# Where the softmax sums of the memory rows stand in an attention segment, and in which array shape they are taken

## The chip, the cores and the metric

The kernel runs on one core of a Trainium2 chip. The metric is the device time of one execution in microseconds (us). The engines of the core have short names here: PE is TensorE (matrix products; PEld is its loading of stationary operands, "weights"), DVE is VectorE, ACT is ScalarE, POOL is GpSimd, SP is SyncE, which issues most transfers. Each engine works through its own instructions in the order of the program; they wait for one another by semaphores.

## The reference

Two kinds of blocks alternate, A, B, A, B, each added to a residual of 2048 rows by 512 columns. B is a gated feed-forward block. A, which the change touches, is a recurrent attention with a memory of 8 rows, run over 64 segments of 32 rows, one after another, with 32 heads of 128 columns:

```python
for s in range(n_seg):
    xs = x[:, s * seg_len:(s + 1) * seg_len, :].copy()
    h = jnp.concatenate([mem, xs], axis=1)
    q = jnp.einsum('btd,dhe->bhte', h, Wq)
    k = jnp.einsum('btd,dhe->bhte', h, Wk)
    v = jnp.einsum('btd,dhe->bhte', h, Wv)
    scores = jnp.einsum('bhqe,bhke->bhqk', q, k) * scale
    scores = jnp.where(mask[None, None], scores, -1000000000.0)
    p = _softmax(scores, axis=-1)
    o = jnp.einsum('bhqk,bhke->bhqe', p, v)
    o = jnp.einsum('bhte,hed->btd', o, Wo)
    mem = o[:, :M, :].copy()
    outs.append(o[:, M:, :])
```

The 8 memory rows of a segment's output are the next segment's memory. So each segment has to wait for the memory rows of the one before it, while its 32 token rows are wanted only later.

## The kernel before

The function `segment(s, ...)` writes one of the 128 segments (64 in each A block). The order on PE, DVE and ACT is the order in which the program names the instructions (`manual_schedule`), so what stands earlier in the code runs earlier on its engine.

The 32 heads are cut into two halves, r = 0 and r = 1, of 16 heads. Within a half the sixteen heads lie in two groups g of 64 partitions. One segment runs as follows; line numbers are those of the profile.

- `qk` (matmuls in `mm_chunk`, L762) projects queries and keys; ACT copies them out (L1087) and DVE turns them (L1090) into QQ and KA. `v_mm` (also L762) projects the values of a half in four parts of four matmuls each, 128 rows by 512 columns, of which four run side by side on 32 columns of the array each. This use of the array is called the 32-column shape below.
- `scores(r)` (L1113, L1117) writes the scores of a half into the PSUM tile psS. `exps(r)` on ACT (L1122) takes their exponential into S, and `close(r)` on DVE (L1125) multiplies with the mask into E[:, r]. E holds, with the keys on the partitions, the unnormalised probabilities.
- The values of half 0 are copied out of PSUM by DVE (L1211, VA[:, 0]), those of half 1 by ACT out of the tile psW (L1226, VA[:, 1]; the profile calls psW psV).
- `fill()` takes the next piece of work that doesn't depend on the segment (projections of a later block, output products of an earlier one): three times in a segment, four matmuls at the first place, eight or four at the second, sixteen or more at the third.
- `pv(r)` multiplies E with the values (L1162, eight matmuls; L1165, two more) into psO[r]. These matmuls take 64 rows of the array each, two side by side, one for each group g: the 64-row shape.
- The softmax's denominators are column sums of E, taken by matmuls with a matrix of ones. `sums_tokens` (L1154, four matmuls, 64-row shape) gives those of the token queries of both halves in the tile psT. For the 8 memory queries half 0 has `sums_zero` (L1136): sixteen matmuls in the 32-column shape with the constant `half`, two for each group and each 32 columns, into columns 224 to 351 of psS. They stand between the third and the fourth part of half 1's values. Half 1 has `sums_one` (L1145): four matmuls in the 64-row shape into columns 320 to 383 of psO[1].
- `inverse(r, src)` makes the reciprocal of the memory sums on ACT as a logarithm (L1179) and an exponential with scale -1 (L1180) into Rm. `memory_out(r)` on DVE (L1183) multiplies psO[r] with it into uT.
- `wo_pairs` (L945) multiplies the memory rows of half 0's sixteen heads with Wo into px, and `wo_rest` (L952) those of half 1. Their sum is the next segment's memory.
- Later ACT inverts the token sums of psT (L1262, L1265) and DVE applies them (L1186, L1189).

The tiles psQ, psS and psT share one place in PSUM (the pool `att`, one buffer): psT can't be written before the last reader of psS is done.

On ACT, between half 1's exponential and the copy of half 1's values, stands half 0's logarithm:

```python
invert = inverse(0, pN.rearrange("p (g q) -> p g q", g=2))
nc.scalar.copy(VA[:, 1].rearrange("p i e -> p (i e)"), psW[:])
invert()
close(1)
```

Where two accesses of a tile touch different banks or columns, the kernel says so by `other_bank`, and no wait is made; so it is for `sums_zero`, which is told not to wait for the exponential of half 1 (`other_bank(sums_zero(pN), expd)`).

Of the kernel before, what the change touches and what calls it, by code (L numbers as in the profile page):

```python
# [7 lines left out]
BF16 = mybir.dt.bfloat16  # L8
# [6 lines left out]
P = 128  # L15
# [52 lines left out]
def _consts(ctx, tc, c, b_sp, between):  # L68
    nc = tc.nc
    cp = ctx.enter_context(tc.tile_pool(name="consts", bufs=1))  # L70
    bsp = cp.tile([P, 16], F32, name="bsp")
    tctx = ExitStack()
    tmp = tctx.enter_context(tc.tile_pool(name="consts_tmp", bufs=1))
    maskf = tmp.tile([P, 224], F32, name="maskf")
    nc.gpsimd.memset(maskf[:], 1.0)
    fourth = tmp.tile([P, 4, 32], F32, name="fourth")
    nc.gpsimd.memset(fourth[:], 0.0)
    nc.gpsimd.affine_select(out=fourth[:], in_=fourth[:], compare_op=ALU.not_equal, fill=1.0,
                            base=0, pattern=[[-1, 4], [-4, 32]], channel_multiplier=1)
    own = maskf[:, 160:224].rearrange("p (i q) -> p i q", i=4)  # L80
    is_own = tmp.tile([P, 4, 1], F32, name="is_own")
    nc.vector.tensor_reduce(out=is_own[:], in_=fourth[:], op=ALU.max, axis=mybir.AxisListType.X)
    nc.vector.tensor_copy(own, is_own[:].to_broadcast([P, 4, 16]))
    between()
    for q in range(0, P, 32):
        blk = maskf[q:q + 32, 0:160].rearrange("p (i q) -> p i q", i=4)[:, :, 8:32]
        nc.gpsimd.affine_select(out=blk, in_=blk, compare_op=ALU.is_ge, fill=0.0, base=8,
                                pattern=[[0, 4], [1, 24]], channel_multiplier=-1)
        last = own[q:q + 32, :, 8:16]
        nc.gpsimd.affine_select(out=last, in_=last, compare_op=ALU.is_ge, fill=0.0, base=0,  # L90
                                pattern=[[1, 4], [4, 8]], channel_multiplier=-1)
    maskN = cp.tile([P, 2, 224], BF16, name="maskN")
    nc.vector.memset(maskN[:], 0.0)
    for gs in range(4):
        nc.vector.tensor_copy(maskN[32 * gs:32 * gs + 32, gs % 2, :], maskf[32 * gs:32 * gs + 32, :])
    ones = cp.tile([P, P], BF16, name="ones")
    nc.vector.memset(ones[:], 1.0)
    half = cp.tile([P, 2, 32], BF16, name="half")
    nc.vector.memset(half[:], 0.0)
    for g in range(2):  # L100
        nc.vector.memset(half[64 * g:64 * g + 64, g, :], 1.0)
    bsp_bf = cp.tile([P, 16], BF16, name="bsp_bf")

    def load_bsp():
        nc.vector.memset(bsp_bf[:], 0.0)
        nc.sync.dma_start(bsp_bf[:], b_sp.rearrange("(t p) -> p t", p=P))
        return lambda: nc.vector.tensor_copy(bsp[:], bsp_bf[:])

    c["bsp"], c["load_bsp"] = bsp, load_bsp
    tctx.close()  # L110
    c.update(maskN=maskN, ones=ones, half=half)
    return c


# [510 lines left out]
def cols_rhs(w, j, kt, cg):  # L625
    at = 2048 * (j % 2) + 512 * cg
    return w[j // 2][:, kt, at:at + 512]
# [90 lines left out]
def a_block(tc, c, rows, front, MV_in, RS_in, MV_out, RS_out, ahead, wo, S, first):  # L718
    nc = tc.nc
    NSEG = S // SEG  # L720
    NB = S // P
    scale = float(DH) ** -0.5
    maskN, ones, half = c["maskN"], c["ones"], c["half"]

    with ExitStack() as ctx:

# [33 lines left out]
        def mm_chunk(ps, lhs, rhs, kts=range(KT)):  # L760

            return [nc.tensor.matmul(ps[32 * cg:32 * cg + 32, :], lhsT=lhs(kt, cg), rhs=rhs(kt, cg), start=(kt == 0), stop=(kt == KT - 1),  # L762
                                     tile_position=(0, 32 * cg)) for kt in kts for cg in range(4)]

        def other_bank(mms, *reads):

            for m in mms:
                for r in reads:
                    tc.declare_no_dep(m.ins, r.ins, reason="another bank of the tile")
# [300 lines left out]
        def segment(s, fill, spare1, spare2, spare3, tail, loads):  # L1070
# [4 lines left out]
            VA = vsp.tile([P, 2, 4, DH], BF16, name="VA")  # L1075
# [6 lines left out]
            E = segp.tile([P, 2, 2, 224], BF16, name="E", bufs=1)  # L1082
# [9 lines left out]
            def v_mm(r, ps, kts=range(KT)):  # L1092
                return mm_chunk(ps, lambda kt, cg: hA_cur[:, kt, :], lambda kt, cg: cols_rhs(w, 4 + r, kt, cg), kts)

            def ends(q):

                return q.rearrange("p h (b e) -> p h b e", e=8)[:, :, 0:5:4, :]
# [5 lines left out]
            def heads40(q):  # L1103
                return q.rearrange("p (i q) -> p i q", q=40)
# [16 lines left out]
            def exps(r):  # L1121
                return nc.scalar.activation(out=S[:, r], in_=psS[:, r, 0:224], func=ACT.Exp, scale=scale)  # L1122

            def close(r):
                nc.vector.tensor_tensor(out=E[:, r], in0=S[:, r].unsqueeze(1).to_broadcast([P, 2, 224]), in1=maskN[:], op=ALU.mult)  # L1125

            def e_all(e, lo, hi):

                return e[:, :, 0:160].rearrange("p n (i q) -> p n i q", q=40)[:, :, :, lo:hi]

            def e_own(e, b):
                return e[:, :, 160:224].rearrange("p n (i b e) -> p n i b e", i=4, b=2)[:, :, :, b, :]

            def sums_zero(pN):

                return [nc.tensor.matmul(pN[32 * cg:32 * cg + 32, 64 * g:64 * g + 64], lhsT=half[:, g, :], rhs=e_own(E[:, 0], 0) if k else e_all(E[:, 0], 0, 8),  # L1136
                                         start=False, stop=True, tile_position=(0, 32 * cg), skip_group_check=True)
                        for k in range(2) for g in range(2) for cg in range(4)]

            def sums_one():  # L1140

                for k in range(2):
                    for g in range(2):
                        e = E[64 * g:64 * g + 64, 1]
                        nc.tensor.matmul(psO[1][:, g, 320:384], lhsT=ones[64 * g:64 * g + 64, :], rhs=e_own(e, 0) if k else e_all(e, 0, 8),  # L1145
                                         start=(k == 0), stop=True, skip_group_check=True)

            def sums_tokens(ps):

# [7 lines left out]
            def pv(r):  # L1157

                for i in range(4):
                    for g in range(2):  # L1160
                        o = psO[r][:, g, 0:320].rearrange("p (s i q) -> p s i q", s=2, i=4)[:, :, i, :]
                        nc.tensor.matmul(o, lhsT=VA[64 * g:64 * g + 64, r, i, :], rhs=E[64 * g:64 * g + 64, r, :, 40 * i:40 * i + 40],  # L1162
                                         start=(r == 0 and i == 0), stop=True, skip_group_check=True)
                for g in range(2):
                    nc.tensor.matmul(ends(heads40(psO[r][:, g, 0:320])), lhsT=VX[64 * g:64 * g + 64, j4, r, :],  # L1165
                                     rhs=E[64 * g:64 * g + 64, r, :, 160:224], start=False, stop=True, skip_group_check=True)
# [10 lines left out]
            def inverse(r, src):  # L1177
                rm = Rm[:, r]
                nc.scalar.activation(out=rm, in_=src, func=ACT.Ln)  # L1179
                return lambda: nc.scalar.activation(out=rm, in_=rm, func=ACT.Exp, scale=-1.0)  # L1180

            def memory_out(r):
                nc.vector.tensor_tensor(out=hview(uT_cur[:], r, 24, 32), in0=oview(r, 0, 8), in1=Rm[:, r].rearrange("p g (n q) -> p g n q", q=8), op=ALU.mult)  # L1183
# [21 lines left out]
            psS = att.tile([P, 2, 512], F32, name="psS")  # L1205
            scores(0)
            expd = exps(0)
# [8 lines left out]
            psW = accB.tile([P, 512], F32, name="psV")  # L1216
            v_mm(1, psW, (0, 1))
            other_bank(scores(1), expd)
            expd = exps(1)
            v_mm(1, psW, (2,))  # L1220
            pN = psS[:, 0, 224:352]
            other_bank(sums_zero(pN), expd)
            v_mm(1, psW, (3,))
            Rm = segp.tile([P, 2, 2, 64], F32, name="Rm", bufs=1)
            invert = inverse(0, pN.rearrange("p (g q) -> p g q", g=2))
            nc.scalar.copy(VA[:, 1].rearrange("p i e -> p (i e)"), psW[:])  # L1226
            invert()
            close(1)

            psO = [attO[r].tile([P, 2, 512], F32, name="psO") for r in range(2)]  # L1230
            if not begin:
                fill()
            pv(0)
            psT = att.tile([P, 2, 512], F32, name="psT")
            sums_tokens(psT)
            sums_one()
            pv(1)
            memory_out(0)
            spare1(E)
            if not begin:  # L1240
# [62 lines left out]
        start = nc.vector if first else nc.gpsimd  # L1303
# [138 lines left out]
        for i in range(H // 2):  # L1442
            for k in range(4):
                h = 2 * i + k % 2
                nc.tensor.matmul(pw[32 * k:32 * k + 32, :], lhsT=ends[k // 2][:, h, :], rhs=wo.head(h).rearrange("p (kt g el) -> p g kt el", kt=4, g=4),
                                 start=(i == 0), stop=(i == H // 2 - 1), tile_position=(0, 32 * k))
# [46 lines left out]
```

## Time and profile before

| | |
|---|---|
| time, median of three runs | 1605.64 us (1602.85 to 1606.57) |
| the profiled execution, device time | 1610.6 us |
| its span in the trace | 1608.9 us |
| PE busy | 1579.1 us (98% of the span) |
| ACT, DVE, POOL busy | 1052.3, 1070.4, 306.5 us |
| the two A blocks, 36 to 697 us and 822 to 1470 us | PE busy 651.3 of 661 us and 643.2 of 648 us |
| granted PE clock | 1.00 in all stretches |

A segment takes some 10 us. In the profile a busy PE only says that some matmul was in flight: a matmul's record is longer than its share of the stream. So the records of four matmuls of 512 columns, 0.40 us, overlap with those of the next four, which start 0.21 us later. What a group costs PE is read from one start to the next, not from the lengths.

A line of the timeline gives the start in us, the length in us, the engine, the line of the kernel, the operation, what it writes and reads with shapes, and how many like it were merged. In brackets is the idle time of the engine before it, and what ended it. Idle time of PEld is not idle time of PE: weights are loaded ahead.

### The profile page before, as it was taken

To read this page: it belongs to the slowest core of one execution; us is meant where nothing else is said; L and a number is where in the kernel's file an instruction comes from. 1 tells how busy PE (TensorE), PEld (TensorE's weight loads), DVE (VectorE), ACT (ScalarE), POOL (GpSimd) and SP (SyncE) were. 2 spreads that over 40 slices of the span, in tenths; PEclk is the share of its full clock that TensorE was granted. 3 is DMA by queue.
4 is the path that set the end of the run, shared out by engine and by line. 5 is a ranking of instruction groups with operands and counts; after the bars stand their busy time and mean duration, and the time that the engine had idled before them with its cause. 6 is when DMAs were issued, how large, how long until landed. Compare 5 with 4: busy or idle time off the path is not lost.

```text
span 1608.9 us, 90911 instructions
## 1 busy us (share of the span) xinstructions
PE 1579.1 (98%) x41021; PEld 981.3 (61%) x41046; DVE 1070.4 (67%) x3066; ACT 1052.3 (65%) x2279; POOL 306.5 (19%) x674
## 2 busy tenths in 40 slices
PE   7899999999999999999999999999999999999999
PEld 3566666666666666666656666666666766665565
DVE  4667766677777776784466666666677667768622
ACT  4677777777777777670057777777777777776400
POOL 6211111112211221320011111111122122224000
PEclk9999999999999999999999999999999999999999
DMA  9322112222311332378952212212233223426698
GB/s 364 131 57 46 40 44 44 50 42 82 80 43 40 87 86 61 106 172 175 209 162 45 48 44 50 44 47 46 73 92 73 47 72 92 97 54 178 143 194 164
DMA packets 255773, 149.67 MB, mean 93 GB/s; under 512 B 188504, under 2 KB 231104, under 8 KB 255384
## 3 DMA queue, kind: packets, MB, share of 16 engines
q1 hardware_dynamic: 241464, 97.68, 27.4%
q0 software_dynamic: 13920, 46.18, 8.9%
q8 instruction: 321, 5.26, 1.4%
q14 instruction: 68, 0.56, 0.1%
HBM read 60.21 MB, written 39.55 MB: 62 GB/s over the span
## 4 chain that ended last, share of the span: by engine, by line
PE 92%; DMA 5%; issue 1%; DVE 1%; ACT 1%; POOL 1%; SPq 0%; POOLq 0%; DVEq 0%; ACTq 0%
PE psQ L762 13%; PE psK L762 13%; PE psb L762 9%; PE pg L403 9%; PE psO L952 7%; PE px L945 7%; PE psm L762 7%; PE psV L762 7%; PE pwB L964 3%; PE psO L1162 3%; PE pz L302 3%; PE py L446 2%; PE psT L1154 2%; PE psS L1113 2%; DMA Wk_sb<-in_A_Wk_dram 1%
## 5 line engine op out<-in xcount | busy, mean ns | idle before, releaser
L762 PEld LDWEIGHTS <-hT 128*32 128x32 bf16 x12288 | 345.3, 96 | 259.2 <-DVE hT L1062 17.7
L762 PE MATMUL psV<-Wv_sb,hT 128*32 128x512 bf16 x2048 | 166.4, 379 | 0.0
L1087 ACT CAST rows<-psQ 128x512 bf16<-128x512 f32 x256 | 145.4, 588 | 23.2 <-PE psQ L762 19.4
L1183 DVE TENSOR_TENSOR uT<-psO,Rm 128x128 bf16<-128x128 f32 x256 | 74.6, 291 | 123.6 <-ACT Rm L1180 123.4
L1090 DVE STREAM_TRANSPOSE QQ<-rows 128x256 f32<-128x256 f32 x256 | 112.5, 439 | 66.2 <-ACT rows L1087 63.6
L1122 ACT ACTIVATE S<-psS 128x224 bf16<-128x224 f32 x256 | 92.2, 360 | 98.1 <-PE psS L1117 98.1
L1090 DVE STREAM_TRANSPOSE KA<-rows 128x256 f32<-128x256 f32 x256 | 113.0, 441 | 64.9 <-ACT rows L1087 62.4
L403 PE MATMUL pg<-z,wspT 128*128 128x344 bf16 x1024 | 154.3, 309 | 0.0
L762 PE MATMUL psK<-Wv_sb,hT 128*32 128x512 bf16 x2048 | 153.2, 378 | 0.0
L1186 DVE TENSOR_TENSOR uT<-psO,Rt 128x384 bf16<-128x384 f32 x256 | 139.9, 547 | 16.4 <-ACT Rt L1265 14.4
L1265 ACT ACTIVATE Rt<-Rt 128x512 f32<-128x512 f32 x256 | 147.3, 622 | 4.0
L952 PE MATMUL psO<-Wo_high,uT 128*32 128x128 bf16 x8192 | 143.0, 219 | 4.1 <-issue 2.2
L762 PE MATMUL psQ<-Wq_sb,hT 128*32 128x512 bf16 x2048 | 136.4, 379 | 0.2 <-issue 0.2
L762 PE MATMUL psQ<-Wk_sb,hT 128*32 128x512 bf16 x2048 | 136.2, 379 | 0.0
L762 PE MATMUL psK<-Wk_sb,hT 128*32 128x512 bf16 x2048 | 136.0, 379 | 0.0
L762 PE MATMUL psm<-Wq_sb,hT 128*32 128x512 bf16 x2048 | 136.0, 379 | 0.0
L945 PE MATMUL px<-Wo,uT 128*32 128x256 bf16 x3840 | 133.8, 273 | 1.3 <-issue 1.2
L952 PEld LDWEIGHTS <-uT 128*32 128x32 bf16 x8192 | 123.6, 97 | 16.2 <-issue 7.8
L403 PEld LDWEIGHTS <-wspT 128*128 128x128 bf16 x1024 | 100.1, 98 | 53.4 <-issue 0.4
L1262 ACT ACTIVATE Rt<-psT 128x1024 f32<-128x1024 f32 x127 | 130.1, 1024 | 3.1
L945 PEld LDWEIGHTS <-uT 128*32 128x32 bf16 x4096 | 104.5, 97 | 25.2 <-issue 2.6
L1044 POOL COPY KX<-old 128x128 bf16<-128x128 bf16 x128 | 65.5, 539 | 263.8 <-PE psS L1117 170.7
(224 smaller groups left out, 2892.9 us busy)
## 6 DMA issues: line engine op xcount, KB each, us to landing
o_d<-o_sb SPq DMA_DIRECT2D x126, 64.0 KB
vb_d<-front SPq DMA_DIRECT2D x31, 256.0 KB
VX<-vb_d SPq DMA_DIRECT2D x124, 64.0 KB
ln_x<-xd SPq DMA_DIRECT2D x26, 256.0 KB
y_o<-o_d POOLq DMA_DIRECT2D x22, 256.0 KB, 3.4
xd<-y_o POOLq DMA_DIRECT2D x22, 256.0 KB, 3.2
Wq_sb<-in_A_Wq_dram POOLq DMA_DIRECT2D x8, 512.0 KB, 7.1
Wk_sb<-in_A_Wk_dram POOLq DMA_DIRECT2D x8, 512.0 KB, 9.3
```

The lines of the kernel that those rows point to most:

```text
L403: nc.tensor.matmul(pg[t][:, k, 0:344], lhsT=wsp[t][:, st, :], rhs=z(st, 344 * k, 344 * k + 344), start=(st == 0), stop=(st == NT - 1))
L762: return [nc.tensor.matmul(ps[32 * cg:32 * cg + 32, :], lhsT=lhs(kt, cg), rhs=rhs(kt, cg), start=(kt == 0), stop=(kt == KT - 1), tile_posi ...
L945: nc.tensor.matmul(px[at:at + 32, 0:256], lhsT=lhs[:, h, :], rhs=wo_rhs(h, slice(k + 2, None, -2) if h % 2 else slice(k, None, 2)), start= ...
L952: nc.tensor.matmul(pw[32 * cg:32 * cg + 32, :], lhsT=lhs[:, h, :], rhs=wo_rhs(h, cg), start=False, stop=(h == H - 1), tile_position=(0, 32 ...
L1044: eng.tensor_copy(KX[r][:].rearrange("p g (k i) -> p i g k", i=4), bs["KTB"][:, r].rearrange("p (i g) k -> p i g k", i=4)[:, :, :, 8 * j4: ...
L1087: return r, mms, copy(r[:].rearrange("p (n el two) -> p n el two", n=8, two=2), ps.rearrange("p (n two el) -> p n el two", n=8, two=2))
L1090: nc.vector.transpose(out=(QQ[:, j % 2, :, 0:32] if j < 2 else KA[:, j % 2]).bitcast(F32).rearrange("p n q one -> p n (q one)"), in_=r[:]. ...
L1122: return nc.scalar.activation(out=S[:, r], in_=psS[:, r, 0:224], func=ACT.Exp, scale=scale)
L1183: nc.vector.tensor_tensor(out=hview(uT_cur[:], r, 24, 32), in0=oview(r, 0, 8), in1=Rm[:, r].rearrange("p g (n q) -> p g n q", q=8), op=ALU ...
L1186: nc.vector.tensor_tensor(out=hview(uT_nxt[:], r, 0, 24), in0=oview(r, 8, 32), in1=rview(r, 0, 24), op=ALU.mult)
L1262: nc.scalar.activation(out=Rt[:], in_=psT[:], func=ACT.Ln)
L1265: nc.scalar.activation(out=rt, in_=rt, func=ACT.Exp, scale=-1.0)
```

## The change

Half 0's memory sums no longer stand between two parts of the values' projection, in sixteen matmuls of the 32-column shape, but as four matmuls of the 64-row shape at the head of the stretch of `pv` and sums, ahead of `pv(0)`. One function, `sums_memory`, serves both halves. The token sums move from the middle of that stretch to its end, behind `pv(1)`. On ACT the copy of half 1's values comes directly after half 1's exponential, and half 0's logarithm and exponential follow it. `close(1)` is named before the sums, `inverse(0)` after `pv(0)`. The declaration that the sums need not wait for the exponential goes, and so does the constant `half`.

```diff
-    half = cp.tile([P, 2, 32], BF16, name="half")
-    nc.vector.memset(half[:], 0.0)
-    for g in range(2):
-        nc.vector.memset(half[64 * g:64 * g + 64, g, :], 1.0)
...
-            def sums_zero(pN):
-
-                return [nc.tensor.matmul(pN[32 * cg:32 * cg + 32, 64 * g:64 * g + 64], lhsT=half[:, g, :], rhs=e_own(E[:, 0], 0) if k else e_all(E[:, 0], 0, 8),
-                                         start=False, stop=True, tile_position=(0, 32 * cg), skip_group_check=True)
-                        for k in range(2) for g in range(2) for cg in range(4)]
-
-            def sums_one():
+            def sums_memory(r, ps, begun):
 
                 for k in range(2):
                     for g in range(2):
-                        e = E[64 * g:64 * g + 64, 1]
-                        nc.tensor.matmul(psO[1][:, g, 320:384], lhsT=ones[64 * g:64 * g + 64, :], rhs=e_own(e, 0) if k else e_all(e, 0, 8),
-                                         start=(k == 0), stop=True, skip_group_check=True)
+                        e = E[64 * g:64 * g + 64, r]
+                        nc.tensor.matmul(ps[:, g, :], lhsT=ones[64 * g:64 * g + 64, :], rhs=e_own(e, 0) if k else e_all(e, 0, 8),
+                                         start=(k == 0 and not begun), stop=True, skip_group_check=True)
...
             expd = exps(1)
-            v_mm(1, psW, (2,))
-            pN = psS[:, 0, 224:352]
-            other_bank(sums_zero(pN), expd)
-            v_mm(1, psW, (3,))
+            v_mm(1, psW, (2, 3))
+            close(1)
+            nc.scalar.copy(VA[:, 1].rearrange("p i e -> p (i e)"), psW[:])
             Rm = segp.tile([P, 2, 2, 64], F32, name="Rm", bufs=1)
-            invert = inverse(0, pN.rearrange("p (g q) -> p g q", g=2))
-            nc.scalar.copy(VA[:, 1].rearrange("p i e -> p (i e)"), psW[:])
-            invert()
-            close(1)
 
             psO = [attO[r].tile([P, 2, 512], F32, name="psO") for r in range(2)]
             if not begin:
                 fill()
+            sums_memory(0, psS[:, :, 224:288], True)
             pv(0)
+            inverse(0, psS[:, :, 224:288])()
+            sums_memory(1, psO[1][:, :, 320:384], False)
+            pv(1)
             psT = att.tile([P, 2, 512], F32, name="psT")
             sums_tokens(psT)
-            sums_one()
-            pv(1)
             memory_out(0)
             spare1(E)
```

## The prediction

> **What bounds the kernel now.** I read the busy times and the chain of work that ended last first:
>
> ```profile
> PE 1579.1 (98%) x41021; PEld 981.3 (61%) x41046; DVE 1070.4 (67%) x3066; ACT 1052.3 (65%) x2279; POOL 306.5 (19%) x674
> ...
> PE 92%; DMA 5%; issue 1%; DVE 1%; ACT 1%; POOL 1%; SPq 0%; POOLq 0%; DVEq 0%; ACTq 0%
> ```
>
> PE is the bound, and 92% of the chain lies on it. So the question is what the change does to PE's stream in one segment, times 128. For that I read the timeline of one ordinary segment, where each line is a group of like instructions:
>
> ```profile
> 344.84 0.68 DVE L1211 CAST VA<-psK 128x512 bf16<-128x512 f32 x1
> ...
> 345.12 0.30 PE L1136 MATMUL psS<-E,half 128*32 128x64 bf16 x16
> 345.17 0.36 ACT L1122 ACTIVATE S<-psS 128x224 bf16<-128x224 f32 x1 [0.75 <-PE psS L1117]
> ...
> 345.24 0.40 PE L762 MATMUL psV<-Wv_sb,hT 128*32 128x512 bf16 x4
> ...
> 345.45 0.40 PE L964 MATMUL pwB<-Wo_high,front 128*32 128x512 bf16 x4
> 345.49 0.28 ACT L1179 ACTIVATE Rm<-psS 128x128 f32<-128x128 f32 x1
> 345.56 0.39 DVE L1125 TENSOR_TENSOR E<-S,maskN 128x448 bf16<-128x448 bf16 x1
> 345.69 0.58 ACT L1226 CAST VA<-psV 128x512 bf16<-128x512 f32 x1
> ...
> 345.79 0.32 PE L1162 MATMUL psO<-E,VA 64*128 64x80 bf16 x8
> ...
> 345.94 0.22 PE L1165 MATMUL psO<-E,VX 64*128 64x128 bf16 x2
> ...
> 346.01 0.45 PE L1154 MATMUL psT<-E,ones 64*128 64x512 bf16 x4
> 346.17 0.31 ACT L1180 ACTIVATE Rm<-Rm 128x128 f32<-128x128 f32 x1
> ...
> 346.30 0.22 PE L1145 MATMUL psO<-E,ones 64*128 64x64 bf16 x4
> ...
> 346.36 0.31 PE L1162 MATMUL psO<-E,VA 64*128 64x80 bf16 x8
> ...
> 346.50 0.22 PE L1165 MATMUL psO<-E,VX 64*128 64x128 bf16 x2
> 346.51 0.29 DVE L1183 TENSOR_TENSOR uT<-psO,Rm 128x128 bf16<-128x128 f32 x1 [0.56 <-ACT Rm L1180]
> ...
> 346.65 0.40 PE L964 MATMUL pwB<-Wo_high,front 128*32 128x512 bf16 x4
> ...
> 346.88 1.04 PE L945 MATMUL px<-Wo,uT 128*32 128x256 bf16 x30
> ```
>
> The reader is to see three things. First, what groups cost from start to start: L1136's sixteen matmuls 0.12 us (345.12 to 345.24), L1145's four 0.06, eight of L1162 0.15, the token sums 0.29, and four fills 0.21. Second, two gaps: from the first fill's end (345.66) to pv(0) 0.13 us, which isn't the wait for half 0's values (their copy ended at 345.52) and which I take as the price of entering the 64-row shape; and at the way out 0.09 (346.50 to 346.65, less 0.06 for two matmuls). Third, how tight half 1 is: E[:, 1] ends at 345.95 and the token sums start 0.06 later; the copy of half 1's values ends at 346.27, and pv(1) starts at 346.36. Between those two events stand the token sums and sums_one: 0.35 us of PE work that need only E.
>
> How long PE takes to go on after a wait is seen in a segment without a first fill:
>
> ```profile
> 77.01 0.11 PEld L1154 LDWEIGHTS <-ones 64*128 64x128 bf16 x4 [0.22 <-DVE E L1125]
> ```
>
> E ended at 76.95 there (started 76.56, 0.39 long), and PE went on at 77.01: 0.06 us.
>
> **The change part by part.**
>
> *Removed: L1136.* Sixteen matmuls, 0.12 us (0.11 in other segments), on PE's path.
>
> The Trainium skill, "TensorE: Matmul & The Clock Gate", section "Wait — 56ns, not 53.3ns?", says that the starts of two matmuls are never closer than about 25 ns however narrow they are. By that the sixteen would take 0.40 us and twelve fewer would save an estimated 0.30 us a segment, 38 us in all; sixteen in 0.12 us is 7.5 ns each, so the trace contradicts it where matmuls run side by side on different columns.
>
> *Added: four matmuls at the head of the stretch.* They have the shape of L1145: 0.06 us. No further change of shape is made, since both neighbours keep theirs. They now wait for half 1's exponential (the declaration is gone): it ends at 345.53, and PE comes to them at 345.33 + 0.21 + 0.13 = 345.67, so that costs nothing; without that 0.08 of cover it would delay pv(0) by as much. Net of both on PE: -0.06 us a segment, -7.7 us in 128, if nothing waits.
>
> *Moved: the copy of half 1's values.* The fourth part of v_mm takes L1136's place at 345.12 and its record ends 0.40 later, at 345.52. ACT starts a copy some 0.05 us after its matmuls (px ends at 347.93 and ACT's copy of it starts at 347.97), and half 1's exponential is off ACT by 345.53, so the copy runs from 345.57 to 346.15, 0.12 earlier than before. With 0.06 pv(1) can start at 346.21.
>
> *Moved: the token sums behind pv(1).* PE comes to the stretch at 345.67, is through half 0's sums at 345.73, through pv(0)'s eight at 345.88 and its two at 345.94. Half 1's sums need E[:, 1]: 345.95 + 0.06 = 346.01, and end at 346.07. Now pv(1) stands next and its values come at 346.21: PE stands for 0.14 us, and the token sums, which could have filled that time, are queued behind the waiting instruction. That is the main term. From there: pv(1)'s two at 346.21 + 0.14 = 346.35, token sums at 346.41, their end at 346.70, the way out 0.09, second fill at 346.79 in place of 346.65: **+0.14 us a segment**.
>
> *Moved: half 0's logarithm.* It now follows the copy on ACT, which starts its next instruction 0.10 before the end of a copy (346.17 against 346.27): 346.05 to 346.33. Two things are queued behind it. psT shares psS's place, so the token sums wait for this logarithm: 346.33 + 0.06 = 346.39 against the 346.41 at which PE comes to them; 0.02 of cover, and past that it adds one for one. And uT of half 0: exponential 346.36 to 346.67, DVE's product 346.70 to 346.99, PE at 347.05. PE comes to px 0.23 after the second fill of four, at 347.02: 0.03 more there; after a fill of eight (0.43) nothing. Half 1's chain isn't last: its logarithm follows pv(1)'s end (346.35 + 0.22 + 0.04 = 346.61), then 0.31, 0.34 and 0.29 from start to start and to the end (346.76, 347.07, 347.41, 347.70 now) bring it to 347.55, and wo_rest comes only at 347.05 + 0.88 = 347.93 (px to wo_rest is 0.88 now). DVE's other work between the two products (0.40 where there is any) fits in as well. Rt, px's folding and the next segment's memory all start from px or wo_rest and shift with them, so nothing behind gives the time back.
>
> *Constants:* three memsets of DVE fewer at the start, off the path: 0. SP's and POOL's queues keep their order; no transfer moves.
>
> **Sum.** I read all segments in the same way (125 of 128 could be read): from the start of L1117 for half 1, the copy's end lies at 1.35 to 1.46 us (median 1.38) and E's at 1.04 to 1.28 (median 1.07). So every segment is like the one shown. In 59 the second fill is of four, in 66 of eight: 59 x 0.17 + 66 x 0.14 = 19.3 us, for 128 segments 19.7. The profiled execution took 1610.6 us, span 1608.9 and 1.7 around it: it would be 1630.3. It lay 5.0 above the median of the three runs, so I forecast 1605.6 + 19.7 = **1625 us**.
>
> **Bounds of the unknown term**, the start of the copy, which the trace before doesn't show without the logarithm ahead of it. Lowest: directly behind the exponential, as the logarithm does now (345.49): it ends at 346.07, pv(1) starts at 346.13, +0.06 a segment, 7.7 us, 1613. Highest: no earlier than now (345.69): pv(1) at 346.33, second fill 0.26 late, px 0.29 late after a short fill, 128 x 0.27 = 35 us, 1641. I take 345.57, because the ACT rows behind PE's records follow them by 0.04 to 0.09.
>
> **The rivals.**
>
> 1. *The matmul saving comes through, 1598 us.* This needs the wait for half 1's values to vanish; it decides from a copy that ends by 346.01, 0.14 earlier than I have it, which is a start at 345.43, before the exponential ahead of it on ACT ends. For it speaks only that PE's queue might run the token sums while pv(1)'s weights wait; I see no matmul overtaking another in the timeline. -0.06 x 128 = -7.7 us. The Trainium skill, "PSUM — Partial Sum Buffer", section "Engine vs sequencer instructions", says that matmuls start and complete in program order, and only weight loads are pulled ahead; no run here shows it. Chance 0.05.
> 2. *The stall is given back, 1605 us.* The memory chain or a transfer would have to be last somewhere in the segment. The waits of PE on DMA and POOL are few (KX three times, 1.6 us), and hT (69 waits of PEld, 17.7 us) comes from wo_rest and shifts. Chance 0.04.
> 3. *The copy gains nothing from the logarithm's leaving, 1641 us*, the upper bound above, with psT's wait on top. For it: before, the copy's start is also exactly where psV's record ends plus 0.05, so the record decides and not the logarithm; against: then it moves with the record. Chance 0.12.
> 4. *A fixed slot for every narrow matmul, 1583 us.* L1145's four take 15 ns each; were that a slot each needs whatever its shape, twelve fewer would give 0.18 us a segment, 23 us. L1136's 7.5 ns each speak against it. Chance 0.01.
>
> That the change doesn't do what it says is excluded by its program: PE's instructions become fewer by 3072, which is twelve matmuls and twelve weight loads in 128 segments.
>
> **How the numbers follow.** The forecast's case has 0.78: 1613, its lowest bound, to 1633, half way to the highest. With rival 3 the slower side reaches 1641. The range is 1612 to 1641; it leaves out the two faster rivals and the given-back stall, 0.10 together, and a little above. A measurement of this kernel can tell 0.2% (3.2 us) from no change. Slower: 0.78 + 0.12 = 0.90; same: 0.04; faster: 0.06.
>
> **What would show it.** In the new profile pv(1)'s weight load (L1162's second group) waits for ACT's copy of VA in nearly all segments, with PE standing 0.14 us before it; the copy starts 0.03 to 0.05 behind psV's record; the token sums follow pv(1) without a gap above 0.05; the four sums of half 0 take 0.06. The forecast is wrong if pv(1) follows half 1's sums at once, if the copy ends more than 0.1 us from 1.27 behind L1117's start, or if a segment's period grows by other than 0.14 to 0.17.

## The result, and the profile after

The changed kernel takes 1617.05 us (median of four runs, 1616.57 to 1618.08) against 1604.64 us of the kernel before (four runs, 1602.85 to 1606.57): a ratio of 1.0078, 95% interval 1.0060 to 1.0095. It is slower by 12.4 us, 0.8%. The forecast was 1625 us, with a range of 1612 to 1641.

The page of the kernel after, its parts 1, 3 and 4 (engines, DMA queues, chain), beside the lines shown of before:

```profile
span 1615.6 us, 87835 instructions
PE 1589.7 (98%) x39485; PEld 969.1 (60%) x39510; DVE 1067.6 (66%) x3063; ACT 1061.7 (66%) x2279; POOL 306.5 (19%) x674
...
q8 instruction: 309, 5.06, 1.3%
...
PE 94%; DMA 3%; issue 1%; ACT 1%; DVE 1%; POOL 0%; POOLq 0%; DVEq 0%; ACTq 0%
```

PE has 1536 matmuls and 1536 weight loads fewer, and its busy time has still grown by 10.6 us: where the records of the matmuls before reach over a gap, a waiting PE counts as busy. The queue that carries instructions (q8) moved 309 packets; before, it moved 321, and that turns out to matter:

```profile
q8 instruction: 321, 5.26, 1.4%
```

The same segment as before, from the timeline of the kernel after (start, length, engine, line, what):

```profile
346.07 0.21 PE L1113 MATMUL psS<-QQ,KX 128*32 128x64 bf16 x4
...
346.76 0.59 ACT L1212 CAST VA<-psV 128x512 bf16<-128x512 f32 x1
...
346.86 0.23 PE L1135 MATMUL psS<-E,ones 64*128 64x64 bf16 x4
...
346.93 0.31 PE L1152 MATMUL psO<-E,VA 64*128 64x80 bf16 x8
...
347.07 0.22 PE L1155 MATMUL psO<-E,VX 64*128 64x128 bf16 x2
...
347.20 0.23 PE L1135 MATMUL psO<-E,ones 64*128 64x64 bf16 x4
347.24 0.28 ACT L1169 ACTIVATE Rm<-psS 128x128 f32<-128x128 f32 x1
...
347.40 0.32 PE L1152 MATMUL psO<-E,VA 64*128 64x80 bf16 x8
...
347.55 0.22 PE L1155 MATMUL psO<-E,VX 64*128 64x128 bf16 x2
...
347.61 0.43 PE L1144 MATMUL psT<-E,ones 64*128 64x512 bf16 x4
...
347.98 0.40 PE L960 MATMUL pwB<-Wo_high,front 128*32 128x512 bf16 x4
...
348.25 1.05 PE L941 MATMUL px<-Wo,uT 128*32 128x256 bf16 x30
```

The reader is to see the step from 347.20 to 347.40. Half 1's four sums need 0.06 us, so pv(1) could start at 347.26; ACT's copy of its values ends at 347.35, and pv(1) starts at 347.40. No idle time stands in brackets there, because the records of the sums, 0.23 us long, reach over the gap: PE's wait has to be read from start to start. The token sums, which need only E and filled this place before, follow at 347.61.

To see all segments, I took from the timelines the time from one half-1 score group (L1117 before, L1113 after) to the next, for 123 pairs of neighbours. This is a segment's period. I split it into a regular part (the period that a fifth of the segments of its kind stay below, for second fills of four and of eight) and what lies above it, the irregular part. Which pairs are taken, and on which side of a step that fifth falls, moves an irregular part by up to some 2 us:

| | period, fill of four | fill of eight | regular, 123 periods | irregular |
|---|---|---|---|---|
| before | 9.67 us | 10.03 us | 1211.4 us | 19.7 us |
| after | 9.86 us | 10.17 us | 1231.7 us | 5.0 us |

The regular part grew by 20.3 us, 21.1 for 128 segments; the forecast had 19.7. But the irregular part fell by 14.7. The profiled spans, 1608.9 and 1615.6, lie 6.7 apart, near 20.3 - 14.7 = 5.6; the medians lie 12.4 apart. So some 9 us of the loss are paid back in a way that the prediction doesn't have. What pays them was the main question for the experiments.

### The profile page after: what moved, and what is told of

It reads as the page before. It is cut to its first block, busy times and chain, and to the rows that moved or that the text cites. A ratio compares the mean times of both kernels' runs of the same rounds, so it can differ in the third digit from the quotient of the medians.

```text
span 1615.6 us, 87835 instructions
## 1 busy us (share of the span) xinstructions
PE 1589.7 (98%) x39485; PEld 969.1 (60%) x39510; DVE 1067.6 (66%) x3063; ACT 1061.7 (66%) x2279; POOL 306.5 (19%) x674
## 4 chain that ended last, share of the span: by engine, by line
PE 94%; DMA 3%; issue 1%; ACT 1%; DVE 1%; POOL 0%; POOLq 0%; DVEq 0%; ACTq 0%
PE psQ L758 13%; PE psK L758 13%; PE psb L758 9%; PE pg L399 9%; PE px L941 7%; PE psO L948 7%; PE psm L758 7%; PE psV L758 7%; PE pz L298 4%; PE pwB L960 3%; PE psO L1152 3%; PE py L442 2%; PE psT L1144 2%; PE psS L1109 2%; PE psS L1135 1%; PE psO L1135 1%
## 5 line engine op out<-in xcount | busy, mean ns | idle before, releaser
L758 PEld LDWEIGHTS <-hT 128*32 128x32 bf16 x12288 | 328.1, 96 | 260.8 <-DVE hT L1058 17.5
L758 PE MATMUL psV<-Wv_sb,hT 128*32 128x512 bf16 x2048 | 150.6, 378 | 0.0
L948 PE MATMUL psO<-Wo_high,uT 128*32 128x128 bf16 x8192 | 137.7, 219 | 1.8 <-DMA Wo_high<-in_A_Wo_dram 1.4
L1040 POOL COPY KX<-front 128x128 bf16<-128x128 bf16 x126 | 64.0, 542 | 267.7 <-PE psS L1113 161.9
```

The costliest lines, as they stand in the source:

```text
L948: nc.tensor.matmul(pw[32 * cg:32 * cg + 32, :], lhsT=lhs[:, h, :], rhs=wo_rhs(h, cg), start=False, stop=(h == H - 1), tile_position=(0, 32 ...
```

## The experiments

Each session has its own runs of the kernel before, and ratios are to those: its medians were 1612.7, 1609.2, 1610.0 and 1610.4 us, all above the 1604.6 of the result's. The periods (in us, after a second fill of four and of eight) and the irregular part (in us) come from each run's trace; in e8 the longer fill is of twelve.

| run | instruction packets | period four / eight | irregular | time | before | ratio, 95% interval |
|---|---|---|---|---|---|---|
| e1_tokens_last | 321 | 9.92 / 10.28 | 7.7 | 1634.78 | 1612.71 | 1.0136 (1.0118 to 1.0155) |
| e2_tokens_ahead_psO | 309 | 9.94 / 10.09 | 5.9 | 1621.63 | 1612.71 | 1.0051 (1.0037 to 1.0065) |
| e3_tokens_ahead | 309 | 9.98 / 10.34 | 4.1 | 1635.68 | 1612.71 | 1.0139 (1.0123 to 1.0156) |
| e5_vx_first | 309 | 9.86 / 10.14 | 8.6 | 1618.69 | 1612.71 | 1.0038 (1.0023 to 1.0052) |
| before_again | 321 | 9.67 / 10.03 | 17.8 | 1612.3, one run | 1609.20 | |
| after_again | 309 | 9.86 / 10.17 | 6.3 | 1618.91 | 1609.20 | 1.0053 (1.0034 to 1.0071) |
| e6_idle_matmuls | 321 | 9.86 / 10.18 | 17.3 | 1634.40 | 1609.20 | 1.0143 (1.0115 to 1.0170) |
| e8_fill_12_16 | 321 | 9.67 / 10.06 | 15.4 | 1612.07 | 1609.20 | 1.0020 (1.0004 to 1.0036) |
| e9_pair18 | 317 | 9.80 / 10.03 | 12.5 | 1614.80 | 1610.01 | 1.0021 (1.0004 to 1.0038) |
| e9_pair20 | 313 | 9.90 / 10.05 | 11.6 | 1619.52 | 1610.01 | 1.0057 (1.0036 to 1.0078) |
| e9_pair22 | 309 | 10.01 / 10.09 | 14.9 | 1629.22 | 1610.01 | 1.0113 (1.0090 to 1.0136) |
| e10_four_zero | 309 | 9.67 / 10.03 | 8.3 | 1599.88 | 1610.44 | 0.9930 (0.9907 to 0.9953) |

### The wait: four orders of the same stretch

*Only the token sums moved, in the kernel before.*

```diff
-            psT = att.tile([P, 2, 512], F32, name="psT")
-            sums_tokens(psT)
             sums_one()
             pv(1)
+            psT = att.tile([P, 2, 512], F32, name="psT")
+            sums_tokens(psT)
```

> The kernel before with one part of the change alone: the token sums (and the tile psT) move behind pv(1); the sixteen narrow matmuls, the order on ACT and the number of PE instructions stay. Main theory (pv(1) waits for ACT's copy of half 1's values once the token sums no longer cover it): the copy ends at 1.38 us after half 1's scores as before, pv(1) starts at 1.44, the token sums at 1.64, the second fill at 2.02 in place of 1.76, so the regular period grows by 0.26 us, 33 us in 128 segments. On the irregular gaps of PE in wo_rest and the fills, put down to 'issue' (some 20 us over the regular periods before, 5 after the change), two theories: if they shrink because PE now stands for a moment in each segment and its instructions can run ahead, they shrink here too and the time is about 1605 + 33 - 8 = 1630; if they shrink because PE has 3072 fewer instructions, they stay and the time is about 1638. A rival that the wait is not on the path would give 1605.

One segment of this run, from half 1's scores on:

```profile
349.26 0.21 PE L1117 MATMUL psS<-QQ,KX 128*32 128x64 bf16 x4
...
350.06 0.58 ACT L1226 CAST VA<-psV 128x512 bf16<-128x512 f32 x1
...
350.70 0.18 PEld L1162 LDWEIGHTS <-VA 64*128 64x128 bf16 x8 [0.20 <-ACT VA L1226]
350.71 0.32 PE L1162 MATMUL psO<-E,VA 64*128 64x80 bf16 x8
...
350.92 0.43 PE L1154 MATMUL psT<-E,ones 64*128 64x512 bf16 x4
...
351.28 0.40 PE L964 MATMUL pwB<-Wo_high,front 128*32 128x512 bf16 x4
```

Counted from half 1's scores, the copy's end lay at 1.38 to 1.39 us, pv(1) at 1.44 to 1.45, the token sums at 1.65 to 1.66 and the second fill at 2.02, as expected to 0.02. The regular periods grew by 0.25, and the time by 22 us (25 were expected if the pause shortens the irregular gaps, 33 if the count of instructions alone does). The wait for the copy is on the path, and this one move makes it; it is the dearest part of the change. In the change itself the earlier copy (end at 1.27) halves it. The irregular part fell from 18 or 20 us to 7.7 though PE has all its instructions, which speaks for the pause.

*The token sums ahead of pv(1) in the kernel after, and half 0's sums in psO[0].*

```diff
-            sums_memory(0, psS[:, :, 224:288], True)
+            sums_memory(0, psO[0][:, :, 320:384], False)
...
             sums_memory(1, psO[1][:, :, 320:384], False)
-            pv(1)
             psT = att.tile([P, 2, 512], F32, name="psT")
             sums_tokens(psT)
+            pv(1)
```

> The changed kernel with the token sums ahead of pv(1) again, and half 0's memory sums in columns 320 to 383 of psO[0] in place of psS, so that psT needn't wait for half 0's logarithm. Main theory: the wait before pv(1) is covered again; half 1's sums are bound by E (1.07 + 0.06) as before, so the second fill is back at 1.76; but half 0's logarithm still follows the copy on ACT, so uT of half 0 comes at 2.11 and px at 2.17: 0.18 late after a second fill of four, nothing after one of eight: 62 x 0.18 = 11 us over before in regular periods. With fewer instructions as the cause of the vanished irregular gaps: about 1605 + 11 - 8 = 1608; with the pause as the cause: about 1616, as after. If the wait before pv(1) weren't the cause of the change's loss, this would be no faster than the changed kernel (1617).

The edit has two lines more: `inverse(0, ...)` reads the new place, and pv(0) adds to psO[0], since the sums now begin it. The second fill is back at 1.76, so the wait before pv(1) is covered. In its place px waits for uT: half 0's logarithm reads the tile that pv(0) also writes, and it now starts at 1.26 (1.17 in the kernel after), 0.04 after the records of pv(0) end at 1.22; so uT ended at 2.20 and not 2.11. So px comes at 2.25 to 2.26 after either fill: 0.27 us late after a fill of four and 0.05 after one of eight. The expected 11 us of regular loss became 20, the time 8.9 us above before. The wait only moved on, from the copy to the logarithm behind it.

*The same with half 0's sums left in psS.*

```diff
             sums_memory(1, psO[1][:, :, 320:384], False)
-            pv(1)
             psT = att.tile([P, 2, 512], F32, name="psT")
             sums_tokens(psT)
+            pv(1)
```

> The changed kernel with the token sums ahead of pv(1), half 0's sums in psS as in the change. Main theory: psT takes psS's place, so the token sums wait for half 0's logarithm, which follows the copy on ACT: they start at 1.51 in place of 1.54, pv(1) at 1.80 in place of 1.33, the second fill at 2.09 in place of 1.90, so 0.19 us a segment more than the changed kernel: about 1617 + 24 = 1641. If psT's place were no matter: as the run with the sums in psO[0].

Token sums at 1.50, pv(1) at 1.77, second fill at 2.08 (1.51, 1.80, 2.09 expected). psT's place in PSUM makes the token sums wait for the logarithm that follows the copy on ACT; so with psS the token sums can't simply go back in front of pv(1). The time is a miss in part: it lay 23 us above the kernel before, where 36 were expected (1641 against 1605), and the periods grew over the changed kernel's by 0.12 after a fill of four and 0.17 after one of eight, not by 0.19.

*pv(1)'s two matmuls that don't need the copy, first.*

```diff
+                if r == 1:
+                    ends_first()
                 for i in range(4):
...
+                if r == 0:
+                    ends_first()
```

> The changed kernel with pv(1)'s two matmuls that don't need ACT's copy (L1155, values of the row block's other columns, VX) ahead of the eight that do. Main theory: they fill 0.055 of the 0.14 us that PE stands, so the second fill comes 0.05 us earlier in each segment: 128 x 0.05 = 6 us, about 1611. Half 0's logarithm (ends 1.45, 1.51 for PE) then becomes the bound of the token sums where pv(1) ends before it, which could leave it at 0.03 to 0.05. If PE isn't waiting for the copy: no change, 1617.

The token sums came at 1.50 to 1.51, where the logarithm lets them, and the second fill at 1.88 in place of 1.90: only 0.02 to 0.03 of the 0.05. The two waits, copy and logarithm, lie so close that taking a part of one hits the other. The time, 1618.69 us, is from another session than the changed kernel's own and can't be told apart from it: 6.0 us above before here, against 9.7 and 12.4 for the change.

### The gaps: instructions or pause

What the irregular part is made of is seen where PE waits for nothing that the profile shows. From the timeline of the kernel before, one segment:

```profile
534.11 0.85 PE L952 MATMUL psO<-Wo_high,uT 128*32 128x128 bf16 x47
535.45 0.45 PE L952 MATMUL psO<-Wo_high,uT 128*32 128x128 bf16 x17 [0.49 <-issue]
```

In the middle of wo_rest, a run of 64 matmuls with no semaphore between, PE stands for 0.49 us and more. The view of waits, PE's rows that end on "issue" (us in total, times, longest), for the kernel before:

```profile
PE psO L952 <- issue: 2.2, 7, 0.5
...
PE px L945 <- issue: 1.2, 2, 0.9
...
PE psb L762 <- issue: 1.1, 3, 0.6
...
PE pwB L964 <- issue: 0.6, 1, 0.6
PE psP L890 <- issue: 0.3, 1, 0.3
PE psQ L762 <- issue: 0.2, 1, 0.2
```

and all of them for the kernel after:

```profile
PE psP L886 <- issue: 0.3, 1, 0.3
```

These waits count only what reaches over the modelled end of the matmul before, so each gap is some 0.2 us longer than its bracket. They fell from 15 to one (in the second pair of traces, before_again and after_again, from 14 to two).

The gaps have a fixed place in the program. The queue of instructions moved 5.26 MB in 321 packets for the 82067 matmuls and weight loads in PE's records, that is 64 bytes an instruction and 256 instructions a packet. For the longest gaps inside wo_rest I counted, in the trace, which instruction of PE's the gap stood before (a matmul for each weight load, and PE's semaphore instructions). In the first trace these were number 30657, 36034, 39106, 44225, 47810, 51393 and 61889, and in e6's, below, 2241, 5825, 18625, 36034, 61890, 67522, 76737 and 78017: modulo 256 all of them are 193 or 194. So PE stands where one block of 256 instructions ends and the next hasn't come. The Trainium skill, "Runtime: NRT & Kernel Launch", section "Instruction fetch mechanics", describes blocks of 256 instructions that the sequencer fetches while it works on the ones before, and calls the cost of crossing mostly hidden; the trace agrees on the blocks, and not on the cost.

The traces also keep when each of these packets moved, and that shows the cause directly. In the kernel before, PE never entered a block less than 1.19 us after the block's packet had ended; in the median it was 2.1 us. From 60 us on, 20 gaps inside wo_rest are over 0.24 us from one weight load to the next, and each of them ends 1.3 to 1.6 us after the end of the packet that PE stood for. PE entered 105 blocks of the kernel before within 1.65 us of their packet's end, and the segments with such a block hold 17.3 of its 20.0 us of irregular time (over all 124 pairs); the kernel after has 45 such blocks, and their segments hold 2.3 us. The packet of a block began, in the median, 0.9 us after PE had entered the block before it, and took 1.1 us. From these numbers a block that PE passes in less than some 0.9 + 1.1 + 1.3 = 3.3 us leaves it standing, which is an estimate.

*As many instructions as before, in the pause of the kernel after.*

```diff
             sums_memory(1, psO[1][:, :, 320:384], False)
+            for _ in range(6):
+                for g in range(2):
+                    nc.tensor.matmul(psO[0][:, g, 320:328], lhsT=ones[64 * g:64 * g + 64, :], rhs=E[64 * g:64 * g + 64, 1, 0, 0:8],
+                                     start=False, stop=True, skip_group_check=True)
             pv(1)
```

> The kernel before itself, for a trace from the chip on which the next three are taken. Both theories: the regular periods are 9.67 us (second fill of four) and 10.03 (of eight) again; what differs from chip to chip are PE's irregular gaps put down to 'issue', 20 us over the regular periods in the first trace.

> The changed kernel itself, beside the next two. Main theory: regular periods 9.86 and 10.17 us (20 us more in all), irregular gaps of some 5 us; the time is that much above before as before's own gaps on this chip leave: 8 to 15 us.

> The changed kernel with twelve narrow matmuls (eight columns each, into columns of psO[0] that nobody reads) and their weight loads put where PE stands idle, between half 1's sums and pv(1): PE then has as many instructions in a segment as before the change. They fit into the 0.14 us if a pair takes up to 0.02, so the regular periods stay at 9.86 and 10.17. If the fewer instructions are why the irregular gaps vanished, the gaps return (from 5 to some 15 us, time 8 to 10 us above the changed kernel); if the pause is why, they stay at 5 to 8 us, and the time within 3 us of the changed kernel.

The twelve fit: pv(1) at 1.33 to 1.34 as in the kernel after, periods 9.86 and 10.18. The irregular part went from 6.3 back to 17.3 us, and the time rose by 15.5 us over the changed kernel's in the same session, beyond the 8 to 10 expected; the irregular part gives 11 of them, and the profiled spans lie 13.1 apart. Here is PE's waiting on issue in it:

```profile
PE psO L948 <- issue: 3.2, 8, 0.8
PE psb L758 <- issue: 2.2, 5, 0.8
...
PE pwB L960 <- issue: 0.4, 1, 0.4
PE psP L886 <- issue: 0.3, 1, 0.3
...
PE psT L1144 <- issue: 0.2, 1, 0.2
```

The trace of before that was taken beside it has 17.8 us, that of the changed kernel 6.3, as in the first. So with the same pause of 0.14 us, filled here, the gaps come and go with the count of instructions.

*Fewer instructions in the kernel before, and nothing else.*

```diff
-                return [nc.tensor.matmul(pN[32 * cg:32 * cg + 32, 64 * g:64 * g + 64], lhsT=half[:, g, :], rhs=e_own(E[:, 0], 0) if k else e_all(E[:, 0], 0, 8),
+                return [nc.tensor.matmul(pN[32 * cg:32 * cg + 32, :], lhsT=ones[:, 0:32], rhs=e_all(E[:, 0], 0, 16),
                                          start=False, stop=True, tile_position=(0, 32 * cg), skip_group_check=True)
-                        for k in range(2) for g in range(2) for cg in range(4)]
+                        for cg in range(4)]
```

> The kernel before with four matmuls of 128 columns in place of sums_zero's sixteen of 64, in the same place and shape; nothing moves. It leaves out the split of half 0's memory sums by groups of heads (the four take other columns of E and add up both groups), so that only the count of instructions changes: 3072 fewer, as many as the change took away, with no wait and no delay added. pv(0) comes 0.05 us earlier, but the token sums still wait for E (1.07 + 0.06), so the regular periods stay at 9.67 and 10.03. If the number of instructions is behind the irregular gaps: they fall from 18 or 20 to about 6 us and the time is 8 to 12 us below before. If only a pause of PE shortens them: as before, within 3 us.

The four matmuls add up both groups of heads, so half 0's memory sums aren't the reference's; the work around them is the same. The periods stayed at 9.67 and 10.03, the irregular part fell to 8.3 us (54 blocks within 1.65 us of their packet's end, 105 before), and the time to 1599.88, 10.6 us below before, inside the 8 to 12 expected. Its waits of PE on issue, all of them:

```profile
PE psO L952 <- issue: 0.4, 2, 0.2
PE pwB L964 <- issue: 0.3, 1, 0.3
```

Together with e6 this settles it from both sides: at equal periods, 3072 instructions more cost 15.5 us and 3072 fewer gain 10.6.

*The same instructions, spread.* In `b_units` and `y_part` four wide matmuls go from the third fill to the second:

```diff
-                for kts in (((0,), (1, 2), (3,)), ((0, 1, 2, 3),))[k % 2 or alone]:
+                for kts in (((0,), (1, 2, 3)), ((0, 1, 2, 3),))[k % 2 or alone]:
...
-                if k in (0, 2):
+                if k in (0, 3):
```

> The kernel before with four wide matmuls moved from the third fill to the second in the segments whose second fill has eight (twelve and sixteen in place of eight and twenty): no wait added, no instruction fewer, but the stretch from the sums to the end of wo_rest, where PE takes most instructions per us, is 0.21 us longer. If PE is short of instructions there, the irregular gaps of these segments shrink (7 us in the first trace, to 2 to 4), against up to 0.06 us a segment that the third fill may be too short for hT: time 0 to 5 us below before. If the gaps have nothing to do with how densely instructions stand: no change or up to 4 us slower.

A miss: wo_rest came 0.22 us later in these segments, their periods grew by 0.03 (by 0.06 if a few segments more are passed over, since the fifth lies at a step), and their irregular part stayed at 7.7 us (7.1 and 9.8 in the two traces of before). The time is 0.2% above before. So it isn't enough that the last stretch is longer. By the times of the packets it is one block at a time that must not pass too fast; why e1's pause of 0.26 us shortened the gaps and these 0.22 us didn't stays open.

*Fewer instructions in another place.* `WO_PAIR`, 16 before, says how many heads go through wo_pairs, at two matmuls in place of four:

```diff
-WO_PAIR = 16
+WO_PAIR = 20
```

> The kernel before with the first 18 heads instead of 16 taken as pairs in wo_pairs (two matmuls of 256 columns for a head in place of four of 128): the same columns for PE, 4 matmuls and 4 weight loads fewer a segment (1024 instructions in all), nothing of the sums touched and no wait added; px ends 0.11 us later, where its sum t1 has 0.23 us to spare before memT. If PE is short of instructions in the dense stretch, fewer of them there shorten the irregular gaps: 2 to 5 us below before. If only a pause of PE helps, no change.

> The same with 20 heads: 2048 instructions fewer, px 0.21 us later, so that t1's 0.23 us are all but used up. Shortage of instructions: gaps of 18 us over the regular periods fall to about 9, time 6 to 10 us below before, regular periods within 0.02 of 9.67 and 10.03, and so faster than both kernels of the study. Pause alone: no change or slower.

> The same with 22 heads: 3072 instructions fewer, as many as the change took away, without its wait. px is 0.32 us later, 0.09 more than t1 has, so the regular periods grow by about 0.09 (11 us) where the third fill doesn't cover it, and the gaps fall to 5 or 6 us: about as before, slower than with 20 heads.

Another miss, in all three: 4.8, 9.5 and 19.2 us slower. The irregular part did fall, to 12.5 and 11.6 us with 18 and 20 heads (14.9 with 22), but the periods with a fill of four grew by 0.13, 0.23 and 0.34, as much as px ended later. The slack that I had read, between t1 (the sum of px's two halves, L1055) and memT (the next memory, L1060), wasn't the one that counts. From the timeline with 20 heads:

```profile
342.66 0.84 PE L952 MATMUL psO<-Wo_high,uT 128*32 128x128 bf16 x48
...
343.27 0.29 DVE L1055 TENSOR_TENSOR t<-px,cross 128x128 f32<-128x128 f32 x1
...
343.62 1.05 PE L762 MATMUL psb<-Wv_sb,hB 128*32 128x512 bf16 x16
```

Where the second fill has four, the third begins in px's place (both are tiles of the pool `accB`), so it waits for the last reader of px, t1: 343.56 plus 0.06 is 343.62, while the last of the 48 matmuls of wo_rest started at 343.28. In the kernel before it is the same:

```profile
348.36 0.29 DVE L1055 TENSOR_TENSOR t<-px,cross 128x128 f32<-128x128 f32 x1
...
348.71 0.61 PE L762 MATMUL psb<-Wq_sb,hB 128*32 128x512 bf16 x8
```

t1 ended at 348.65, the last matmul of wo_rest had started at 348.62, and the third fill began at 348.71. So px had no slack in these segments.

No version that computes the whole reference beat the kernel before; e10 suggests that some 10 us would be there for one that needs twelve matmuls fewer without a later px, copy or logarithm.

## Why the prediction was right, and what it left out

- *The wait of pv(1) for ACT's copy* is as predicted: the copy from 0.69 to 1.28 after half 1's scores (0.69 to 1.27 worked out), pv(1) at 1.33 (1.33), PE standing 0.14. e1 shows that moving the token sums makes it; e2 shows that covering it brings the second fill back.
- *Behind it*: token sums at 1.54 (1.53), second fill at 1.91 (1.91), px 2.18 (2.17) after a fill of four, 2.34 (2.34) after eight. The extra 0.03 by uT after a short fill was predicted and came. So did the tight place of psT: e3 and e5 show it as the next bound.
- *The sum for the path*, 19.7 us, against 21.1 measured in the periods. They grew by 0.19 after a fill of four and 0.14 after one of eight, so after short fills the growth lies 0.02 outside the 0.14 to 0.17 that the prediction allowed itself. The traces hold 62 and 64 such segments, not 59 and 66 of 125, which moves the sum by 0.1 us.
- *The mis-sized step is "Removed: L1136"*, priced at 0.12 us of PE's stream a segment. Net of the four matmuls added, it also took 24 instructions a segment out of PE's program, a gain that the sum put at nothing. What is missing from the regular loss is 8.7 us in the result's session (21.1 less 12.4) and 11.4 in the second (21.1 less 9.7); e10, which takes out as many instructions and moves nothing, gained 10.6. PE's rows on "issue" in the waits of before (15 gaps, 5.6 us beyond the records) were there to be read; I counted the waits on DMA, POOL and DVE and passed them over. PEld's rows on "issue" don't tell it: they grew from 32 to 55 us with the change.
- *Rival 2* (given back behind, 0.04) thus had its sign right and its mechanism wrong: neither the memory chain nor a transfer of the kernel's data, but the transfer of the program itself. *Rival 1* fell: the token sums overtook the waiting pv(1) in none of 128 segments. *Rival 3* fell with the copy's start: it moved by 0.11 to 0.12, as the fourth part's record did (in e10, with the logarithm still ahead of the copy, both moved by 0.06). *Rival 4* fell too: by it PE would have saved 0.18 us a segment, and pv(0) came only 0.05 earlier, at 0.86 after half 1's scores in place of 0.91.
- With e10's gain taken off, the forecast would have been 1625 - 10.6 = 1614 us, 3 below the time measured; without it, it was 8 us too high. That it still lies inside the range is owed to the range's width of 29 us, and in that it was lucky: the range was drawn for the start of the copy and not for this effect.

## What to carry to other kernels

Work that looks movable may be the cover of a wait: before moving it, read what the engine behind it will find unready, and then what is second and third to be late (here copy, logarithm and uT, at 1.33, 1.51 and 2.18 us after half 1's scores, each within 0.15 us of PE's own pace). On PE, busy throughout, the number of instructions was a cost of its own here beside their durations; look for waits on "issue" in runs of instructions without semaphores, and test it by adding as many idle instructions in a place where the engine stands anyway. A change that is right in what it removes can be wrong in what it reorders: e10's removal without reordering gained nearly what the change lost, though with sums that aren't the reference's.

## What the runs showed of the hardware that I had not expected

In the traces of the kernel before PE lost some 16 to 17 us of some 1210 in the A blocks' periods because its program came too late, in gaps up to 1.2 us long at the borders of blocks of 256 instructions, in a kernel with 82067 matmuls and weight loads in 1609 us. Each block's packet began, in the median, 0.9 us after PE had entered the block before it, so the program came about one block ahead. The longest gaps stand in or near runs like wo_rest, where 128 instructions pass in 0.86 us. The times vary too: runs of the kernel before went from 1602.85 to 1619.42 us over the sessions, those of the changed kernel from 1616.57 to 1622.05; that the gaps make this spread isn't shown.
